# A fused attention and ELU-MLP kernel: preparing w_in moves to GpSimd, w_out is prepared two tiles at a time, the ELU is rewritten with a Relu on ScalarE, and the opening's order of work is new

## The chip, the cores and the metric

The kernel runs on one NeuronCore of a Trainium2 chip. The number that counts is the device time of one execution in microseconds (us). The engines are written as the profile names them: PE is TensorE (matmuls), PEld its weight loads, DVE VectorE, ACT ScalarE, POOL GpSimd, SP SyncE, which here only issues DMAs.

## The reference

`q`, `k` and `v` have shape (8 images, 12 heads, 448 tokens, 64) in float32. `w_in` (768 x 2048) and `w_out` (2048 x 768) come in float64, 12.6 MB each.

```python
scores = scale * np.matmul(q, k.transpose(0, 1, 3, 2)) - np.log(S)
attn = 1.0 / (1.0 + np.exp(-scores))
attn_out = np.matmul(attn, v)                       # sigmoid attention, no softmax
x = attn_out.transpose(0, 2, 1, 3).reshape(B * S, H * D)      # 3584 x 768
h = x @ w_in
g = np.where(h > 0.0, h, np.exp(np.minimum(h, 0.0)) - 1.0)    # ELU
out = g @ w_out
```

## The kernel before

**Arithmetic.** Most operands are split into a float16 high part and a float16 low part ("high" is a scaled copy on ACT, "low" is source times scale minus high on DVE, helper `low`, L186). A product is then three float16 matmuls. Only the six head pairs of image 0 are kept in float32 (`EXACT`); they are turned on PE (L483) and copied out of PSUM on DVE (`copied`, L490).

**Tiling.** The work goes by image. Per image there are six pairs of heads: `scores` (L549) gives a PSUM tile of 128 keys by 2 x 448 queries, `sigmoid` (L557) reads it on ACT, `values` (L619, L607) multiplies it with v, and `finish_high` and `finish_low` put the result into `xh`, the input of the MLP. The first layer (`moe1`, products at L723) walks over 16 tiles of 128 hidden units, 18 matmuls each, into PSUM tiles `ph`. For each, ACT takes the exponential (L733), DVE builds the ELU from it in two steps (L739, L740), ACT writes the high part of `g` (L746) and DVE its low part (L186). The second layer (`moe2`, L785) multiplies `g` with `w_out` into tiles of 128 tokens by 384 outputs, evicted on DVE (L795) and sent by SP (L799).

**The opening.** The weights must be turned from float64 into float16 pairs. A tile of 128 hidden units of w_in goes through these steps, one letter each in the string `ORDER`: `i` DMA of the raw words into a spare place of `wo` or `g` (L248); `A` two ACT passes, the top word's magnitude and the last bits (L202, L207); `B` DVE joins them (L211); `C` PE sums of magnitudes (L220); `D` a scale, by DVE and one small POOL step (L276, L141, L145); `E` DVE puts the sign back (L227); `F` ACT writes the high part (L288); `G` DVE the low part (L186, tile name `wi`). The float32 tile between `A` and `G` lies in one of five places (`stage`, `WT = 5`): the field of tile f+5 cannot start before `G` of tile f is done. w_out has the same steps in 32 tiles of 384 (`o`, `H` to `N`), staged in spare places of `wo` and in the buffers `at` and `o`.

**What sets the order.** The Tile layer here does not reorder: each engine runs its instructions in the order in which they are recorded, waiting on semaphores. In the opening that order is written out by hand: every letter of `ORDER` advances one generator of `streams`. The opening takes in all of image 0's and image 1's attention, all weights, and image 0's first and second layer (`m`, `x`, `y`, `z`, `w`, `p`). From the first layer of image 1 on, the order comes from the loop at the end of the kernel: the first layer of image b, then the attention of image b+1 with the matmuls of image b's second layer as filler between its steps.

## Time and profile before

| what | value |
|---|---|
| time of the runs | 1171.29 us median of 3 (1170.32 to 1171.38) |
| the profiled execution's own time | 1171.42 us |
| its span, first to last instruction | 1169.6 us |
| PE, PEld busy | 1141.7 us (98%), 635.5 us (54%) |
| DVE, ACT, POOL busy | 785.4 us (67%), 705.7 us (60%), 179.6 us (15%) |
| DMA | 92.12 MB, mean 79 GB/s; 254 to 266 GB/s in the first two slices of 29 us |

The two layers after the opening repeat for seven images at a PE that is busy throughout, so the page's shares over the whole span say little about the opening. The opening has to be cut out with windows: up to the first matmul of image 0's first layer, from there to the first of image 1's first layer, and the rest. An instruction's duration includes its pipeline's start and end, and neighbours on one engine overlap by some 0.08 us, so sums of durations are a little more than busy time.

### The profile page before, as it was taken

How to read it: one execution, taken by the hardware profiler on the slowest of the kernel's cores; microseconds unless marked ns; L12 is line 12 of the kernel's file. 1: busy time of each engine (PE TensorE's matmuls, PEld its weight loads, DVE VectorE, ACT ScalarE, POOL GpSimd, SP SyncE). 2: the span in 40 equal slices, each digit the busy share in tenths (PEclk: the TensorE clock that was granted, in tenths of full speed). 3: DMA queues.
4: the chain of work that ended last, by engine and by line, in shares of the span. 5: the costliest groups of instructions: out<-in, count | busy, mean ns of one | idle time of the engine just before them, and what ended most of it. 6: DMA issues, size and time to landing. Idle time of an engine off the chain costs nothing.

```text
span 1169.6 us, 23893 instructions
## 1 busy us (share of the span) xinstructions
PE 1141.7 (98%) x9662; PEld 635.5 (54%) x9662; DVE 785.4 (67%) x1506; ACT 705.7 (60%) x1087; POOL 179.6 (15%) x491
## 2 busy tenths in 40 slices
PE   5989999999999999999999999999999999999998
PEld 2335464555665555655666555655566555555565
DVE  6999988866666667866666666767576575855400
ACT  6987779746664368844766348845666446764300
POOL 1233212210220102211120111301022010300000
PEclk9999999999999999999999999999999999999999
DMA  9986445311242113512044121622134131310000
GB/s 254 266 259 209 124 98 112 86 41 42 63 95 63 41 42 78 120 28 62 19 99 96 38 50 42 110 55 52 39 84 92 37 60 30 73 36 1 1 27 27
DMA packets 219150, 92.12 MB, mean 79 GB/s; under 512 B 182688, under 2 KB 214944, under 8 KB 219040
## 3 DMA queue, kind: packets, MB, share of 16 engines
q1 hardware_dynamic: 219040, 90.61, 32.4%
q8 instruction: 75, 1.23, 0.4%
q14 instruction: 35, 0.29, 0.1%
HBM read 60.29 MB, written 11.01 MB: 61 GB/s over the span
## 4 chain that ended last, share of the span: by engine, by line
PE 81%; DVE 3%; ACT 2%; issue 1%; DMA 0%; POOL 0%; DVEq 0%; ACTq 0%; POOLq 0%
PE ph L723 33%; PE po L785 29%; PE pav L619 7%; PE psc L549 6%; PE po_r L785 5%; PE pscr L649 1%; ACT sg L557 1%; DVE wo L186 1%; DVE g L186 1%; DVE at L186 0%; DMA so<-in_moe_w_out_dram 0%; ACT at L587 0%; DVE nat L186 0%; ACT nat L501 0%; DVE mx L193 0%
## 5 line engine op out<-in xcount | busy, mean ns | idle before, releaser
L723 PE MATMUL ph<-xh,wi 128*128 128x448 f16 x2304 | 440.3, 352 | 1.0 <-DVE wi L186 0.9
L785 PE MATMUL po<-wo,g 128*64 128x384 f16 (+1 forms) x4320 | 393.0, 327 | 0.8 <-DVE e L740 0.5
L785 PEld LDWEIGHTS <-g 128*64 128x64 f16 (+1 forms) x4992 | 291.3, 109 | 160.1 <-issue 30.3
L723 PEld LDWEIGHTS <-wi 128*128 128x128 f16 x2304 | 223.4, 98 | 211.7 <-issue 3.7
L733 ACT ACTIVATE e<-ph,msc 128x448 f32<-128x448 f32 x128 | 81.0, 633 | 198.1 <-PE ph L723 168.4
L186 DVE SCALAR_TENSOR_TENSOR at<-sg,at 128x896 f16<-128x896 f32 x120 | 127.6, 1090 | 106.5 <-ACT at L587 106.5
L739 DVE TENSOR_SCALAR e<-e 128x448 f32<-128x448 f32 x128 | 50.1, 391 | 128.7 <-ACT e L733 128.7
L557 ACT ACTIVATE sg<-psc,bias,sc 128x896 f32<-128x896 f32 x126 | 133.9, 1094 | 3.1
L587 ACT ACTIVATE at<-sg 128x896 f16<-128x896 f32 x120 | 109.6, 947 | 0.7
L626 ACT ACTIVATE xh<-pav,sc 128x448 f16<-128x448 f32 x48 | 30.3, 632 | 127.7 <-PE pav L619 122.6
L746 ACT ACTIVATE g<-e,msc 128x384 f16<-128x384 f32 (+1 forms) x192 | 96.0, 533 | 6.7 <-DVE e L740 4.1
L186 DVE SCALAR_TENSOR_TENSOR g<-e,msc,g 128x384 f16<-128x384 f32 (+1 forms) x192 | 94.6, 522 | 0.4
L740 DVE SCALAR_TENSOR_TENSOR e<-ph,msc,e 128x448 f32<-128x448 f32 x128 | 87.5, 684 | 5.1
L549 PE MATMUL psc<-qk 64*128 64x448 f16 x756 | 86.3, 351 | 0.1
L145 POOL TENSOR_SCALAR sc<-sc 128x3 f32<-128x3 f32 (+1 forms) x48 | 11.7, 244 | 432.4 <-DVE pw L178 432.3
L619 PE MATMUL pav<-at,vn 128*64 128x448 f16 x720 | 75.6, 353 | 0.0
L619 PEld LDWEIGHTS <-vn 128*64 128x64 f16 x880 | 49.8, 110 | 32.2 <-issue 1.8
L785 PE MATMUL po_r<-wo,g 128*64 128x384 f16 (+1 forms) x672 | 64.9, 326 | 0.0
L186 DVE SCALAR_TENSOR_TENSOR nat<-raw,sc,nat 128x384 f16<-128x384 f32 (+1 forms) x126 | 60.0, 525 | 1.7 <-ACT nat L501 0.9
L501 ACT ACTIVATE nat<-raw,sc 128x384 f16<-128x384 f32 (+1 forms) x126 | 59.8, 531 | 1.3 <-POOL sc L145 0.9
L186 DVE SCALAR_TENSOR_TENSOR xh<-pav,sc,xh 128x448 f16<-128x448 f32 x48 | 32.6, 680 | 40.7 <-ACT xh L626 40.7
L795 DVE TENSOR_SCALAR o<-po,osc 128x384 f32<-128x384 f32 x48 | 29.3, 610 | 42.3 <-PE po L785 36.4
(120 smaller groups left out, 979.4 us busy)
## 6 DMA issues: line engine op xcount, KB each, us to landing
wo<-in_moe_w_in_dram SPq DMA_DIRECT2D x14, 768.0 KB, 6.3
raw<-in_q_dram SPq DMA_DIRECT2D x48, 192.0 KB, 3.9
raw<-in_k_dram SPq DMA_DIRECT2D x48, 192.0 KB, 3.4
rv<-in_v_dram SPq DMA_DIRECT2D x48, 192.0 KB, 3.0
out_dram<-o SPq DMA_DIRECT2D x48, 192.0 KB, 2.1
wo<-in_moe_w_out_dram SPq DMA_DIRECT2D x18, 384.0 KB, 3.8
so<-in_moe_w_out_dram SPq DMA_DIRECT2D x14, 384.0 KB, 3.7
rv<-in_v_dram SPq DMA_DIRECT2D x96, 32.0 KB, 2.5
```

Of the source, the lines that this page charges most:

```text
L186: nc.vector.scalar_tensor_tensor(lo, src, s, hi, op0=ALU.mult, op1=ALU.subtract)
L501: nc.scalar.mul(self.nat[:, 0, t : t + n], src, s)
L549: nc.tensor.matmul(psc[:, j, :S] if g < NC else psc[rows[j], 0, :S], kk[rows[j], o], qq[rows[j], :S], start=(n == 0), stop=(n == len(parts ...
L557: nc.scalar.activation(to, psc, AF.Sigmoid, bias=bias, scale=self.s_scale)
L587: nc.scalar.mul(hi, sg, 2.0**ATOP)
L619: nc.tensor.matmul(pav[rows[j], :S], vv[i][:, 2 * NC + j if g == NC else j * NC + g], sg[k][:, j], start=(g == 0 and n == 0), stop=(g == N ...
L723: nc.tensor.matmul(self.ph[f], wi[:, wj, c, f * P : (f + 1) * P], self.xh[c][:, xj], start=(n == 0), stop=(n == 3 * NK - 1),)
L733: nc.scalar.activation(self.e[f], self.ph[f], AF.Exp, scale=self.m[:, 0, f : f + 1])
L739: nc.vector.tensor_scalar(e, e, 1.0, -1.0, op0=ALU.min, op1=ALU.add)
L740: nc.vector.scalar_tensor_tensor(e, self.ph.pop(f), self.m[:, 0, f : f + 1], e, op0=ALU.mult, op1=ALU.max)
L746: nc.scalar.mul(g[:, 0, f, o : o + n], self.e[f][:, i : i + n], self.m[:, 1, f : f + 1])
L785: nc.tensor.matmul(po[r, :HM], tokens[:, r], wo[:, i, f, wj], start=(n == 0), stop=(n == 3 * NF - 1),)
```

## The change

The edits, by what they do:

- **w_in (F, G).** The staged float32 tile is scaled in place on POOL (`tensor_scalar`), copied into the high part on POOL (`tensor_copy`), and the low part is the difference of the two, on POOL again (`tensor_tensor`). ACT's scaled copy and DVE's `low` on w_in are gone.
- **Turned float32 pairs (e).** The copy out of PSUM for image 0's six pairs is made by ACT instead of DVE.
- **w_out (H to K).** Loads, fields, magnitudes, sums and signs take two 128-row tiles at once: 16 DMAs of 768 KB and 16 steps of 768 columns where 32 DMAs of 384 KB and 32 steps of 384 were. The splits (M, N) still go tile by tile. Raw words are staged in spare places of `wo` and `g` and, at the end, in `ats`.
- **ELU.** After the exponential, ACT computes Relu(c - c * exp(h)) in place, c being the inverse of the scale; DVE then takes max(h, 0) minus that in one step. The DVE step with `min` and `add` (L739) is gone. The scale table `msc` has three rows instead of two, each made by POOL, and `high` and `low` of g now use one scale per token image (`xr`) for all tiles.
- **Last keys of image 0.** The last 64 keys of two pairs share one PSUM tile, as for the other images.
- **Buffers.** `at` and `o` become fixed tiles (`ats`, `room`) with three places each.
- **End.** In the last image the tile of leftover tokens comes first in each half; the very last tile is evicted in two halves, DVE and ACT, each sent from its own queue (SP and ACT).
- **Order.** `ORDER` is another string, and k of the very first pair is loaded from ACT's queue.

```diff
 ORDER = (
-    "iiqviiqviAAAABCDEiBadbCFGcDeSEAABSCFGEiAABDCaDETTFSbSWTATAdWWWqviiFAXAAAGceBCSGEDBYYSCEa"
+    "iiiiiqqvvAAAAAAAAAABCDEBCEiiFGBDCDFEFGGBBCDCadCadbcEDEeSFGFGbceSTTASWWSTABAABSWCiiqiTAATD"
...
     def w_in_high():
         for f in range(NF):
-            nc.scalar.mul(wi[:, 0, :, f * P : (f + 1) * P], staged(f), w_in_scale[f])
+            t = staged(f)
+            nc.gpsimd.tensor_scalar(t, t, w_in_scale[f], None, op0=ALU.mult)
+            nc.gpsimd.tensor_copy(wi[:, 0, :, f * P : (f + 1) * P], t)
             yield
     def w_in_low():
         for f in range(NF):
             d = wi[:, :, :, f * P : (f + 1) * P]
-            low(d[:, 1], staged(f), w_in_scale.pop(f), d[:, 0])
+            nc.gpsimd.tensor_tensor(d[:, 1], staged(f), d[:, 0], op=ALU.subtract)
             yield
...
+                src = w_out[f * 2 * P : (f + 1) * 2 * P, i * HM : (i + 1) * HM]
+                nc.sync.dma_start(st, src.rearrange("(a p) c -> p a c", a=2))
...
+            issue = nc.scalar if i and b + hp == 0 else nc.sync
...
         def copied(self):
             qk = early[:, self.hp % 2]
-            nc.vector.tensor_copy(qk, self.pt[:, : 2 * S])
+            nc.scalar.copy(qk, self.pt[:, : 2 * S])
...
+        def missing(self, f):
+            e = self.e[f]
+            nc.scalar.activation(
+                e, e, AF.Relu, bias=self.m[:, 1, f : f + 1], scale=self.m[:, 2, f : f + 1]
+            )
         def elu(self, f):
             e = self.e[f]
-            nc.vector.tensor_scalar(e, e, 1.0, -1.0, op0=ALU.min, op1=ALU.add)
             nc.vector.scalar_tensor_tensor(
-                e, self.ph.pop(f), self.m[:, 0, f : f + 1], e, op0=ALU.mult, op1=ALU.max
+                e, self.ph.pop(f), 0.0, e, op0=ALU.max, op1=ALU.subtract
             )
...
+        def evict_halves():
+            (pp, dst), = dsts
+            turns["o"] += 1
+            o, h = room[:, turns["o"] % OB], HM // 2
+            nc.vector.tensor_scalar(o[:, :h], po[:, :h], sc(), None, op0=ALU.mult)
+            nc.scalar.mul(o[:, h:], po[:, h:HM], sc())
+            nc.sync.dma_start(dst[:, i * HM : i * HM + h], o[pp, :h])
+            nc.scalar.dma_start(dst[:, i * HM + h : (i + 1) * HM], o[pp, h:])
```

In what follows, line numbers of the changed kernel differ from those of before: L292, L293 and L299 are POOL's scale, copy and subtraction, L205 and L210 are ACT's field and last bits (L202 and L207 before), L560 is the sigmoid, L629 is `finish_high`, L747 the Relu.

The first place is POOL's queue at the start. Before, it holds only scales (`ws`, `sc`, `pw`, `xs`), one number a partition:

```order
L145 TENSOR_SCALAR ws<-ws 128x1
L145 TENSOR_SCALAR sc_0_157<-sc_0_157 128x1
L181 TENSOR_SCALAR pw_0_156<-pw_0_156 128x1
L418 COPY xs_164<-pw_0_156 128x1
L419 COPY xs_164<-sc_0_157 128x1
L421 TENSOR_SCALAR sc_0_157<-xs_164 128x1
L145 TENSOR_SCALAR ws<-ws 128x1 x3
```

Now three w_in tiles, nine instructions of 768 columns, stand ahead of the scales of the first pair:

```order
L148 TENSOR_SCALAR ws<-ws 128x1
L292 TENSOR_SCALAR g<-g,ws 128x768
L293 CAST wi<-g 128x6x128
L299 TENSOR_TENSOR wi<-g,wi 128x6x128
L148 TENSOR_SCALAR ws<-ws 128x1 x2
L292 TENSOR_SCALAR g<-g,ws 128x768
L293 CAST wi<-g 128x6x128
L292 TENSOR_SCALAR g<-g,ws 128x768
L293 CAST wi<-g 128x6x128
L299 TENSOR_TENSOR wi<-g,wi 128x6x128 x2
L148 TENSOR_SCALAR ws<-ws 128x1
L148 TENSOR_SCALAR sc_0_221<-sc_0_221 128x1
```

Each tile has become three wide instructions in this queue, in line with the small ones. Up to the field of the last w_in tile, eleven tiles must have passed.

The second place is ACT's queue at the end of image 0's attention (`psc` and `pscr` are score tiles, `pt` a turned pair, `xh` the MLP's input, `g<-wo` or `wo<-wo` 128x768 a weight tile). Before, from the fifth pair's high part (`pav_4`) to the sixth's:

```order
L626 ACTIVATE xh_173<-pav_4_662,sc_4_605 128x448
L557 ACTIVATE sg_5_762<-psc_5_738,bias 128x896
L202 ACTIVATE wo<-wo 128x384
L207 ACTIVATE wo<-wo 128x384
L557 ACTIVATE sg_5_766<-psc_5_741,bias 128x896
L557 ACTIVATE sg_5_792<-psc_5_782,bias 128x448
L202 ACTIVATE wo<-wo 128x384
L207 ACTIVATE wo<-wo 128x384
L202 ACTIVATE wo<-wo 128x384
L626 ACTIVATE xh_173<-pav_5_785,sc_5_689 128x448
```

Now, from the field of the last (16th) w_in tile on:

```order
L205 ACTIVATE g<-wo 128x768
L210 ACTIVATE wo<-wo 128x768
L560 ACTIVATE sgr_4_706<-pscr_4_694,bias 128x448
L560 ACTIVATE sg_5_739<-psc_5_717,bias 128x896
L629 ACTIVATE xh_239<-pav_4_665,sc_4_609 128x448
L210 ACTIVATE g<-g 128x768
L560 ACTIVATE sg_5_788<-psc_5_782,bias 128x896
L560 ACTIVATE sg_5_790<-psc_5_785,bias 128x896
L205 ACTIVATE wo<-wo 128x768
L210 ACTIVATE wo<-wo 128x768
L205 ACTIVATE wo<-wo 128x768
L629 ACTIVATE xh_239<-pav_5_792,sc_5_682 128x448
```

The scaled copies of w_in (L288) have left this queue and the copies of turned pairs (`pt`, L494) have come in further up. The last pair's high part still stands behind a fixed list of weight passes, and the 16th field now stands behind POOL's eleventh subtraction.

The third place is the end: SP's last DMAs before, of the leftover tokens (two parts),

```order
L799 DMA out_0_dram<-o7_2_1_14529 128x384
L799 DMA out_0_dram<-o7_r_1_14581 64x384 x2
```

and ACT's last rows now, its half of the last eviction and the DMA of it:

```order
L821 ACTIVATE room_72<-po7_2_1_14283,osc6_12340 128x192
L823 DMA out_0_dram<-room_72 128x192
```

SP has the other half, one DMA of 128 rows by 192 columns, instead of two DMAs one after the other.

More of the change, by code (lines that the diff above doesn't have):

```diff
@@ L103, in attention_ffn @@
     early = early.rearrange("p (n x) -> p n x", n=2)
+    ats = const.tile([P, AB, 2, 2, S], F16, name="ats")
+    turns = {"at": 0, "o": 0}
+    room = const.tile([P, OB, HM], F32, name="room")
     wp = const.tile([P, NF], F32, name="wp")
@@ L376, in w_out_low @@
             s = w_out_scale[i][:, 1 + f : 2 + f]
[L377 removed]
+            low(wo[:, i, f, 1], w_out_whole[i, f // 2][:, f % 2], s, wo[:, i, f, 0])
             yield
@@ L386, in load_qk @@
         for i, src in enumerate((q, k)):
-            nc.sync.dma_start(
+            issue = nc.scalar if i and b + hp == 0 else nc.sync
+            issue.dma_start(
                 raw[:, i * (NC + 1) :][:, :NC],
@@ L390, in load_qk @@
             )
-            nc.sync.dma_start(
+            issue.dma_start(
                 raw[rows[i], NC], src[b, h0 : h0 + 2, SM:].rearrange("h r d -> r h d")
@@ L549, in scores @@
                     nc.tensor.matmul(
-                        psc[:, j, :S] if g < NC else psc[rows[j], 0, :S],
-                        kk[rows[j], o], qq[rows[j], :S],
+                        psc[:, j, :S], kk[rows[j], o], qq[rows[j], :S],
                         start=(n == 0), stop=(n == len(parts) - 1),
@@ L559, in soften @@
         def soften(self, g):
-            nb = 2 if g < NC else 1
             psc = self.psc.pop(g)
             sg = sb.tile([P, 2, S], F32, tag="sg", name=f"sg{g}{self.u}", bufs=SB)
-            self.sigmoid(sg[:, :nb], psc[:, :nb, :S])
+            self.sigmoid(sg, psc[:, :, :S])
             self.sg[g] = [sg]
@@ L584, in high @@
             (sg,) = self.sg[g]
-            at = sb.tile([P, 2, 2, S], F16, tag="at", name=f"at{g}{self.u}", bufs=AB)
+            at = ats[:, turns["at"] % AB]
+            turns["at"] += 1
             hi, lo = at[:, 0], at[:, 1]
@@ L643, in last_keys @@
         o = slice(S, S + R)
-        for n in range(3):
+        terms = 2 * len(two[0].qk) - 1
+        for n in range(terms):
             for i, p in enumerate(two):
-                hi, lo = p.qk
+                hi, lo = p.qk[0], p.qk[-1]
                 kk, qq = [(hi, hi), (lo, hi), (hi, lo)][n]
@@ L773, in moe1, with moe2_tile @@
         x.parts(NF - 1)
-    def moe2_tile(dsts, lh, sc, i, u, halves, out_later=None):
+    def moe2_tile(dsts, lh, sc, i, u, halves, out_later=None, last=False):
         cols = slice(i * HM, (i + 1) * HM)
@@ L793, in evict @@
         def evict():
-            o = sb.tile([P, HM], F32, tag="o", name=f"o{u}", bufs=OB)
+            turns["o"] += 1
+            o = room[:, 2 if turns["o"] <= NC else turns["o"] % OB]
             nc.vector.tensor_scalar(o, po[:, :HM], sc(), None, op0=ALU.mult)
@@ L831, in tokens, with tile_of @@
             return out[b * S + SM : (b + 1) * S]
-        def tile_of(c, i):
+        def tile_of(c, i, last):
             if c < NC:
@@ L846, in moe2 @@
         for i in range(NH):
-            for c in range(NC + j):
-                yield from tile_of(c, i)
+            tiles = list(range(NC + j))
+            if b == B - 1:
+                tiles = tiles[NC:] + tiles[:NC]
+            for c in tiles:
+                yield from tile_of(c, i, b == B - 1 and (c, i) == (NC - 1, NH - 1))
     pairs = [(b, hp) for b in range(B) for hp in range(NP)]
@@ L950, in scores @@
             p = pair_of(n)
-            for t in range(NC + (n < FIRST)):
+            for t in range(NC):
                 p.scores(t)
@@ L954, in scores @@
                 yield
-            if n >= FIRST and n % 2 == 0:
+            if n % 2 == 0:
                 two = pair_of(n), pair_of(n + 1)
@@ L1005, in layer @@
         xp, xr, last = next(whole)
-        m = sb.tile([P, 2, NF], F32, tag="msc", name=f"msc{b}")
+        m = sb.tile([P, 3, NF], F32, tag="msc", name=f"msc{b}")
         def first():
@@ L1095, in attention_ffn @@
         "m": first_layer("products"), "x": first_layer("exponential"),
-        "y": first_layer("elu"), "z": first_layer("high"), "w": first_layer("low"),
+        "l": first_layer("missing"), "y": first_layer("elu"), "z": first_layer("high"), "w": first_layer("low"),
         "p": output_products(), "k": evictions(),
```

119 lines of the change are left out of this document (59 added, 60 removed).

## The prediction

> **What bounds the kernel now.** I cut the span by windows at three instants: the first `ph` matmul of image 0 (85.3 us), the first of image 1 (226.8), and PE's end (1165.4). The columns are the window, its length, busy time of PE, PEld, DVE, ACT and POOL with instruction counts, PE clock, DMA share and GB/s.
>
> ```profile
> 0.00:30.00 30.00, 17.10 (x82) 7.98 (x84) 18.20 (x36) 18.41 (x23) 5.17 (x23) 0.94 0.94 253
> 30.00:85.30 55.30, 47.77 (x266) 18.21 (x263) 52.45 (x108) 50.06 (x71) 16.07 (x41) 0.97 0.97 273
> 85.30:226.80 141.50, 138.22 (x1166) 76.16 (x1166) 132.02 (x263) 115.60 (x194) 35.07 (x72) 1.00 0.51 127
> 226.80:1165.40 938.60, 938.57 (x8154) 533.14 (x8153) 582.10 (x1101) 521.62 (x801) 123.32 (x356) 1.00 0.25 55
> 1165.40:1169.60 4.20, 0.00 (x0) 0.00 (x0) 0.62 (x1) 0.00 (x0) 0.00 (x0) 0.92 0.20 47
> ```
>
> From 226.8 us on PE is idle for 0.03 of 938.6 us, so nothing on another engine can shorten that stage; it can only lengthen it. From 85.3 to 226.8 PE is idle for 3.3 us. Before 85.3 PE has little to do that is ready; there DVE (52.45 of 55.30 us), ACT (50.06) and the DMA engines (0.97) are all nearly full. After it, PE has a fixed list: 16 tiles of the first layer, the second layer and image 1's attention. So the time is the instant of the first `ph` matmul, plus a list that PE works off almost without a gap, plus the tail. PE's timeline shows that instant and the next one:
>
> ```profile
> 85.28 3.56 PE L723 MATMUL ph<-xh,wi 128*128 128x448 f16 x18
> 226.78 3.58 PE L723 MATMUL ph<-xh,wi 128*128 128x448 f16 x18
> ```
>
> **What the change does before 85.3 us.** By lines, up to that instant, first ACT's groups and then DVE's (count, busy us, mean ns, idle before):
>
> ```profile
> L557 ACT ACTIVATE sg<-psc,bias 128x896 f32<-128x896 f32 x18 | 17.6, 1000 | 0.6 <-PE psc L549 0.6
> L202 ACT ACTIVATE g<-wo 128x768 f32<-128x768 f32 x14 | 12.6, 899 | 6.1 <-DMA wo<-in_moe_w_in_dram 6.1
> L288 ACT ACTIVATE wi<-g,ws 128x768 f16<-128x768 f32 x12 | 11.1, 929 | 2.9 <-POOL ws L145 2.8
> ...
> L202 ACT ACTIVATE wo<-wo 128x384 f32<-128x384 f32 x6 | 3.3, 556 | 0.0
> ```
> ```profile
> L227 DVE SCALAR_TENSOR_TENSOR g<-wo,g 128x768 uint32<-128x768 uint32 x14 | 13.3, 953 | 1.5 <-PE si L220 1.5
> L211 DVE SCALAR_TENSOR_TENSOR g<-g,wo 128x768 uint32<-128x768 uint32 x14 | 13.3, 954 | 6.0 <-ACT wo L207 5.9
> L186 DVE SCALAR_TENSOR_TENSOR wi<-g,ws,wi 128x768 f16<-128x768 f32 x11 | 11.1, 1012 | 0.0
> L490 DVE COPY g<-pt 128x896 f32<-128x896 f32 x6 | 6.5, 1084 | 2.9 <-PE pt L483 2.9
> ```
>
> DVE loses 11.1 + 6.5 = 17.6 of 70.7 us and stops being a bound. ACT loses 11.1 us of scaled copies and gains six copies out of PSUM; this ACT form is not in the trace, but a sigmoid of the same size from PSUM is (17.6 / 18 = 0.98 us), so +5.9. A w_out field of two tiles costs one 768-wide pass (0.90) where two of 0.56 were, a gain of 0.2 a pass, which in this stage, with about ten passes, is some 0.4 us after overlap. ACT goes from 68.5 to 62.9 us. If ACT paced the stage at the same busy share, the instant would be 85.3 x 62.9 / 68.5 = 78.3: 7.0 us earlier.
>
> POOL sets the other bound. A tile of w_in now takes three of its instructions, and the field of tile 16 on ACT waits for the subtraction of tile 11. No POOL instruction this wide is in the trace. The nearest rows:
>
> ```profile
> 0.72 0.10 POOL L88 MEMSET bias<- 128x1 f32 x1 [0.29 <-POOLq L1201]
> 0.75 0.20 POOL masks.py:197 MEMSET ident<- 128x128 f32 x1
> 1.31 0.29 POOL masks.py:199 TENSOR_SCALAR_AFFINE_SELECT ident<-ident 128x128 f32<-128x128 f32 x1
> 13.18 0.22 POOL L181 TENSOR_SCALAR pw<-pw 128x1 f32<-128x1 f32 x1
> ```
>
> From 1 to 128 columns a memset grows by 0.10 us, 0.8 ns a column; the select, which also reads, by 1.5 ns at most. With 0.2 us fixed, 768 columns are 0.84 us at the one rate and 1.36 at the other. I take 0.84 for scale and copy, and for the subtraction, with two inputs read in turn, twice the column rate: 1.5. A tile then takes 3.2 us when nothing disturbs it (2.5 if the second input is free, 5.2 at the select's rate throughout). The Trainium skill (GPSIMD Engine Reference, Elementwise — side-by-side cycle accounting) gives 4.5 us for a two-input add of 2048 float32 columns; an estimate by it is 1.7 us for the subtraction, and the tile would be 3.4 us.
>
> It is disturbed. In the steady stage POOL's small steps and DVE's stand so in time (start, length; POOL, then DVE):
>
> ```profile
> 304.28 1.19 POOL L465 COPY sc<-sc 64x1 f32<-64x1 f32 x2
> 305.57 0.64 POOL L467 TENSOR_SCALAR sc<-pw 128x1 f32<-128x1 f32 x1
> 306.31 0.59 POOL L415 TENSOR_SCALAR xs<-xs,pw 128x1 f32<-128x1 f32 x1
> ```
> ```profile
> 304.34 1.09 DVE L186 SCALAR_TENSOR_TENSOR at<-sg,at 128x896 f16<-128x896 f32 x1 [0.54 <-ACT at L587]
> 305.46 1.27 DVE L577 SCALAR_TENSOR_TENSOR ar<-sgr,ar 64x448 f16<-64x448 f32 x2
> ```
>
> A POOL step of about 0.2 us that meets a DVE step with two SBUF inputs ends just after that step does (305.47 after 305.43; 306.21 after 306.1, the end of the first of the two at 305.46): it waits for the rest of it. The Trainium skill (SBUF — State Buffer, Summary: rules for kernel authors) says that whichever of the two starts second is blocked entirely; the trace agrees for POOL behind DVE (1.19 us for two steps of 0.2), and no run here shows the other direction with a long POOL step. This speaks against the change: magnitudes and signs (L211, L227) are such DVE steps, 34.6 us of them before 85.3 with the w_out ones. The wait per POOL instruction lies between nothing and one whole DVE step (0.95 us), so 0 to 2.85 a tile. DVE spends 34.6 of 85 us, 0.4, in such steps, and the mean rest of one is 0.47, which gives 0.6; with DVE often eager, I take 1.1. The tile is then 4.3 us (2.5 to 8.1 between the far ends).
>
> POOL can start where the first scaled copy does now (10.4 us), and 31 small steps stand in its queue up to the eleventh subtraction, at 0.33 us each (21.24 us in 64 instructions before 85.3) 10.3 us. The rows of that start and of the last pair's high part, which stands 2.9 us ahead of the first `ph`:
>
> ```profile
> 10.40 0.94 ACT L288 ACTIVATE wi<-g,ws 128x768 f16<-128x768 f32 x1 [1.01 <-POOL ws L145]
> ...
> 82.35 0.64 ACT L626 ACTIVATE xh<-pav,sc 128x448 f16<-128x448 f32 x1 [2.58 <-PE pr L171]
> ```
>
> Eleven tiles end at 10.4 + 11 x 4.3 + 10.3 = 68.0 us. From the 16th field ACT has eleven passes to the last pair's high part (six weight passes of 0.9, three sigmoids of 1.0, one of 0.6 and one high part of 0.6), 8.8 us after overlap, and it waits for PE's value products there, which I take as the 2.58 us of now: 79.4. With the 2.9 us that follow the instant is 82.3, **-3.0 us**. POOL, not ACT, sets it.
>
> **After it.** DVE is busy for 132.0 of 141.5 us and loses 16 ELU steps (0.39 each, 6.2 us), the last five low parts of w_in (4.7) and some 4 us by w_out's wider steps. ACT is at 115.6; it gains 16 Relus and loses four scaled copies and about 5 us of fields. A Relu of 448 columns I price like the exponential, 0.64:
>
> ```profile
> L733 ACT ACTIVATE e<-ph,msc 128x448 f32<-128x448 f32 x112 | 71.1, 635 | 194.6 <-PE ph L723 167.0 <-PE pr L171 25.9 <-POOL msc L697 1.4
> L739 DVE TENSOR_SCALAR e<-e 128x448 f32<-128x448 f32 x112 | 43.9, 392 | 128.7 <-ACT e L733 128.7
> ```
>
> Both stay under PE's list, and at most PE's 3.3 us of idling come back. I take **-1.0**. Bounds: -3.3, and +3 if new waits of the same kind open.
>
> In the steady stage ACT gains 112 x 0.635 = 71 us and DVE loses 43.9. ACT would be at 593 of 938.6. For each `ph` tile ACT has exponential, Relu and high part, 1.9 us (2.2 where the high part is in two), against PE's 3.56 for the 18 matmuls; the ELU's chain grows by 0.24 us under the two tiles that PE is ahead. **0**. Without that lead it would cost 0.24 x 112 = 27 us. POOL's third step per image delays only the first Relu of an image, behind three further `ph` tiles. The buffers `ats` and `room` keep three places.
>
> **The tail.**
>
> ```profile
> 1165.41 0.62 DVE L795 TENSOR_SCALAR o_r<-po_r,osc 128x384 f32<-128x384 f32 x1 [7.18 <-PE po_r L785]
> 1166.05 1.11 SPq L799 DMA_DIRECT2D out_dram<-o_r  x2
> ```
>
> Half of the eviction lies between 0.31 and 0.62; at 0.45 it saves 0.17. The second issue, half of 1.11, goes to ACT's queue: 0.55. **-0.7** (0 to -0.9).
>
> **Sum.** Against the profiled execution's 1171.4: -3.0 - 1.0 + 0 - 0.7 = -4.7, so 1166.7; its time is 0.13 above the median of the runs, so **1166.6**.
>
> **The rivals.**
>
> *A. POOL is later, and the change is slower.* If every POOL instruction meets a whole DVE step, a tile is 6.05 us, eleven end at 87.3, and the first `ph` comes at 101.6: +16.3. Break-even is at 4.6 us a tile. For a middle value of 5.2, the instant is 92.2, +6.9; with the tail's -0.7: 1177.5. For it speaks 1.19 us for two short copies above; against it, DVE's lower load. Its mirror, DVE held up by POOL, makes fields and signs late and ends the same.
>
> *B. POOL is quick and meets few DVE steps.* At 3.2 us a tile ACT is the bound at 78.3; with the most of the rest (-7.0 - 2.0 - 0.7) this gives 1161.6. For it speaks that DVE's load falls by a quarter (17.6 of 70.7 us), so that fewer POOL steps find it busy; against it, that what stays on DVE is mostly of the two-input kind.
>
> *C. No change.* The DMA engines are at 0.97 up to 85.3 us and their bytes are the same. Five w_in tiles now go ahead of the first q, so the first sigmoid comes later than now and ACT's gain is eaten by its early idling (6.1 us already wait for w_in): the instant stays, and with the tail 1170.
>
> **How the numbers follow.** The forecast has 0.42, B 0.13, C 0.18, A 0.27. About 0.2% (2.3 us) is what a measurement of this kernel tells from no change: faster 0.55, same 0.18, slower 0.27. The range is 1159 to 1178: from a little beyond B, if PE's idling comes back in full, to A's middle value; A's far end is left out. The likeliest case alone has 1163 to 1169.
>
> **What would show it.** Right: the first `ph` near 82; wide POOL steps of 0.8 to 1.7 us whose ends lie just behind DVE steps; ACT's fields waiting for POOL's subtraction; PE without a gap from image 1 on; a tail near 3.5 us. Wrong: a tile over 4.6 us, DVE's signs stretched beyond 0.95 us, the first sigmoid much after 18 us, or PE waiting for the ELU.

## The result, and the profile after

The changed kernel takes 1193.72 us (median of 4 runs, 1192.79 to 1193.87); the kernel before, run beside it, takes 1171.34. The ratio is 1.0186, with a 95% interval of 1.0173 to 1.0200. It is slower, by 22 us, where 5 us less had been forecast. The profiled execution took 1192.79 us with a span of 1191.0.

These are the windows of the changed kernel, cut at the same events as in the prediction: 30 us, the first `ph` matmul of image 0, the first of image 1, PE's end, the end. The columns are those of the prediction's first table.

```profile
0.00:30.00 30.00, 13.85 (x85) 8.04 (x86) 16.86 (x34) 18.56 (x23) 20.50 (x23) 1.00 0.98 275
30.00:103.85 73.85, 51.33 (x260) 19.36 (x258) 45.34 (x83) 46.54 (x58) 69.96 (x72) 0.83 0.71 191
103.85:247.43 143.58, 139.94 (x1171) 74.85 (x1169) 126.94 (x218) 118.45 (x180) 51.71 (x94) 0.99 0.49 120
247.43:1186.80 939.37, 939.37 (x8154) 533.16 (x8153) 535.11 (x991) 605.36 (x913) 123.18 (x363) 1.00 0.25 56
1186.80:1191.00 4.20, 0.02 (x1) 0.00 (x0) 0.42 (x1) 0.42 (x1) 0.00 (x0) 1.00 0.16 49
```

The first `ph` matmul starts at 103.85 us instead of 85.28, 18.6 us later. From there to image 1's first the kernel takes 2.1 us more (143.6 against 141.5), the steady stage 0.8 more (939.4 against 938.6), the tail 0.05 less. The sum, 21.4, is the difference of the spans (1191.0 and 1169.6). In the second window DVE and ACT are no longer full (45 and 47 of 74 us), nor is DMA (0.71, before 0.97). POOL is: 69.96 of 73.85 us.

POOL's wide steps, by lines over the whole run (count, busy us, mean ns, idle before), and the small scale that every w_in tile needs, by lines from 0 to 120 us:

```profile
L292 POOL TENSOR_SCALAR g<-g,ws 128x768 f32<-128x768 f32 x16 | 39.8, 2485 | 0.6
L299 POOL TENSOR_TENSOR wi<-g,wi 128x768 f16<-128x768 f32 x16 | 30.0, 1887 | 0.7
L293 POOL CAST wi<-g 128x768 f16<-128x768 f32 x16 | 16.3, 1020 | 1.1
```
```profile
L148 POOL TENSOR_SCALAR ws<-ws 128x1 f32<-128x1 f32 x16 | 9.6, 601 | 9.3 <-DVE ws L144 8.0
```

A tile takes 2485 + 1020 + 1887 = 5392 ns of POOL. The chain of waits of the changed kernel up to the first `ph`, in order of time (start, length, work), runs through POOL almost without a break from 33.5 to 95 us. Its end:

```profile
84.79 2.23 POOL wi L299
...
88.74 2.97 POOL g L292
91.78 0.97 POOL wi L293
92.83 0.80 POOL ws L148
...
94.75 0.27 POOL xs L420
...
95.32 2.11 DVE xh L676 x4
...
99.76 2.10 DVE wo L214
101.86 0.60 DVE xh L189
```

The eleventh subtraction ends at 87.02. Then the scale and copy of a later tile stand in POOL's queue ahead of the last pair's small steps (`ws` at 92.83 to `xs` at 94.75). DVE's rescaling of the other five parts of `xh` (L676) waits for those, and the last low part (L189) stands behind it in DVE's queue, with a w_out step between them (99.76) that takes 2.10 us, more than twice its usual 0.95, beside a subtraction on POOL. The waits up to 110 us say who stands behind POOL:

```profile
PE si L223 <- DVE g L214: 20.9, 7, 8.2
DVE g L214 <- ACT wo L210: 20.7, 6, 6.0
ACT g L205 <- POOL wi L299: 16.4, 5, 6.1
```

The columns are us in total, times and longest. ACT's field waits for POOL's subtraction 16.4 us, DVE's magnitudes wait for ACT, and PE's sums for DVE: one wait, passed on twice.

PE's timeline around the first `ph`, and two windows that show its clock (the third number from the end) there:

```profile
102.51 1.44 PE L223 MATMUL so<-wo,ones 128*128 128x384 bf16 x4 [5.69 <-DVE xh L189]
103.85 4.98 PE L730 MATMUL ph<-xh,wi 128*128 128x448 f16 x18
```
```profile
100.00:105.00 5.00, 2.49 (x9) 1.11 (x9) 4.93 (x7) 1.51 (x2) 5.00 (x3) 0.50 0.24 58
105.00:110.00 5.00, 5.00 (x24) 2.44 (x23) 4.90 (x9) 1.07 (x1) 4.76 (x4) 0.83 0.57 157
```

PE was idle for 5.69 us, its granted clock was 0.50 and then 0.83, and the first 18 `ph` matmuls took 4.98 us where 3.56 stood before. That is 1.4 of the 2.1 us lost between the two first `ph`.

### The profile page after: what moved, and what is told of

Read it like the earlier page. It is cut to its first block, busy times and chain, and to the rows that moved or that the text cites. A ratio compares the mean times of both kernels' runs of the same rounds, so it can differ in the third digit from the quotient of the medians.

```text
span 1191.0 us, 23762 instructions
## 1 busy us (share of the span) xinstructions
PE 1144.5 (96%) x9662; PEld 635.4 (53%) x9662; DVE 724.7 (61%) x1324; ACT 789.3 (66%) x1174; POOL 265.3 (22%) x550
## 4 chain that ended last, share of the span: by engine, by line
PE 85%; POOL 5%; DVE 4%; ACT 3%; DMA 2%; issue 1%; SPq 0%; DVEq 0%; POOLq 0%; ACTq 0%
PE ph L730 32%; PE po L796 31%; PE pav L622 7%; PE psc L553 7%; PE po_r L796 5%; POOL g L292 2%; POOL wi L299 1%; PE pscr L653 1%; POOL wi L293 1%; DVE wo L230 1%; DMA wo<-in_moe_w_in_dram 1%; DMA qk<-nat 1%; DVE wo L214 1%; POOL ws L148 0%; DVE mx L196 0%
## 5 line engine op out<-in xcount | busy, mean ns | idle before, releaser
L753 DVE SCALAR_TENSOR_TENSOR e<-ph,e 128x448 f32<-128x448 f32 x128 | 79.6, 622 | 183.2 <-ACT e L747 183.2
L189 DVE SCALAR_TENSOR_TENSOR ats<-sg,ats 128x896 f16<-128x896 f32 x120 | 127.4, 1089 | 104.4 <-ACT ats L590 104.4
L560 ACT ACTIVATE sg<-psc,bias,sc 128x896 f32<-128x896 f32 x126 | 133.7, 1093 | 5.9 <-PE psc L553 2.7
L629 ACT ACTIVATE xh<-pav,sc 128x448 f16<-128x448 f32 x48 | 30.3, 631 | 121.3 <-PE pav L622 120.0
L590 ACT ACTIVATE ats<-sg 128x896 f16<-128x896 f32 x120 | 109.5, 947 | 0.6
L747 ACT ACTIVATE e<-e,msc 128x448 f32<-128x448 f32 x128 | 97.4, 761 | 4.4
L759 ACT ACTIVATE g<-e,rr 128x384 f16<-128x384 f32 (+1 forms) x192 | 95.4, 531 | 2.7 <-DVE e L753 2.2
L189 DVE SCALAR_TENSOR_TENSOR g<-e,rr,g 128x384 f16<-128x384 f32 (+1 forms) x192 | 95.5, 527 | 0.4
L622 PE MATMUL pav<-ats,vn 128*64 128x448 f16 x720 | 75.9, 353 | 0.5 <-DVE xh L189 0.5
L189 DVE SCALAR_TENSOR_TENSOR nat<-raw,sc,nat 128x384 f16<-128x384 f32 (+1 forms) x126 | 60.6, 529 | 1.5 <-ACT nat L505 0.7
L452 POOL TENSOR_TENSOR mx<-mx,half 128x2 bf16<-128x2 bf16 x42 | 10.5, 250 | 218.5 <-DVE mx L196 211.7
L189 DVE SCALAR_TENSOR_TENSOR xh<-pav,sc,xh 128x448 f16<-128x448 f32 x48 | 32.6, 680 | 43.0 <-ACT xh L629 43.0
```

The source lines that it names most:

```text
L189: nc.vector.scalar_tensor_tensor(lo, src, s, hi, op0=ALU.mult, op1=ALU.subtract)
L560: nc.scalar.activation(to, psc, AF.Sigmoid, bias=bias, scale=self.s_scale)
L590: nc.scalar.mul(hi, sg, 2.0**ATOP)
L622: nc.tensor.matmul(pav[rows[j], :S], vv[i][:, 2 * NC + j if g == NC else j * NC + g], sg[k][:, j], start=(g == 0 and n == 0), stop=(g == N ...
L747: nc.scalar.activation(e, e, AF.Relu, bias=self.m[:, 1, f : f + 1], scale=self.m[:, 2, f : f + 1])
L753: nc.vector.scalar_tensor_tensor(e, self.ph.pop(f), 0.0, e, op0=ALU.max, op1=ALU.subtract)
```

## The experiments

The theory that the profile suggests, P: POOL's time per tile of w_in sets the first `ph`. Rivals: the new order itself is worse (O); what counts is that POOL's wide steps hold DVE up (D); the Relu form costs (R). "First `ph`", "image 0" (from the first `ph` to image 1's first) and "steady" are from the profiled execution of each run, in us; the time is the median. POOL's time per tile is the sum of the mean durations of its wide steps. The interval is that of the ratio to runs of the kernel before taken beside it. e14's profiled execution is the slowest of its ten (1174.8).

| run | order | w_in on POOL | time | ratio (95%) | first `ph` | image 0 | steady |
|---|---|---|---|---|---|---|---|
| before | old | nothing | 1171.3 | | 85.3 | 141.5 | 938.6 |
| the change | new | all, 5.39 us a tile | 1193.7 | 1.0173 to 1.0200 | 103.8 | 143.6 | 939.4 |
| e2 | old | all, 5.24 | 1197.6 | 1.0215 to 1.0247 | 104.8 | 148.9 | 938.6 |
| e17 | old | every second tile | 1182.9 | 1.0075 to 1.0114 | 93.4 | 145.5 | 938.6 |
| e18 | old | every fourth tile | 1176.0 | 1.0023 to 1.0053 | 87.4 | 144.6 | 938.6 |
| e5 | new | narrow scale, 3.89 | 1178.6 | 1.0039 to 1.0088 | 89.9 | 143.2 | 939.4 |
| e6 | new | narrow scale and subtraction, 2.67 | 1166.9 | 0.9945 to 0.9969 | 81.6 | 141.9 | 939.4 |
| e1 | new | nothing | 1191.2 | 1.0159 to 1.0198 | 100.2 | 145.6 | 939.4 |
| e16 | new | every fourth tile | 1188.4 | 1.0131 to 1.0165 | 99.3 | 144.5 | 939.4 |
| e15 | new | every second tile | 1187.7 | 1.0123 to 1.0153 | 96.6 | 147.1 | 939.4 |
| e11 | new | nothing, all on DVE | 1180.5 | 1.0060 to 1.0108 | 93.5 | 141.2 | 939.4 |
| e14 | old | nothing; Relu alone | 1172.1 | 1.0001 to 1.0024 | 87.0 | 142.4 | 939.4 |

**Is POOL alone enough? (e2)** The kernel before, in its old order, with only w_in's three steps put on POOL:

```diff
-            nc.scalar.mul(wi[:, 0, :, f * P : (f + 1) * P], staged(f), w_in_scale[f])
+            t = staged(f)
+            nc.gpsimd.tensor_scalar(t, t, w_in_scale[f], None, op0=ALU.mult)
+            nc.gpsimd.tensor_copy(wi[:, 0, :, f * P : (f + 1) * P], t)
...
-            low(d[:, 1], staged(f), w_in_scale.pop(f), d[:, 0])
+            nc.gpsimd.tensor_tensor(d[:, 1], staged(f), d[:, 0], op=ALU.subtract)
```

> The kernel before with one part of the change alone: w_in's scale, copy and subtraction on GpSimd, in the old order. Theory P: eleven tiles at 5.4 us and the small steps end near 80 us and the old order was not made for that; the first ph comes at 96 to 108 us and the time is 1182 to 1195 us. Rival O: the first ph stays within 4 us of 85.3, the time under 1176 us.

It took 1197.6 us. POOL's lines up to 105 us, and PE's row of the first `ph`:

```profile
L289 POOL TENSOR_SCALAR g<-g,ws 128x768 f32<-128x768 f32 x13 | 31.7, 2437 | 0.6
L296 POOL TENSOR_TENSOR wi<-g,wi 128x768 f16<-128x768 f32 x11 | 19.2, 1753 | 0.5
L290 POOL CAST wi<-g 128x768 f16<-128x768 f32 x12 | 12.6, 1051 | 0.8
```
```profile
104.77 5.24 PE L725 MATMUL ph<-xh,wi 128*128 128x448 f16 x18
```

The first `ph` comes 19.5 us late without any other part of the change, and the time is a little beyond P's upper end. POOL alone is enough.

**How much of it does POOL bear? (e17, e18)** The same, but only the odd tiles (e17), or only tiles 3, 7, 11 and 15 (e18), go to POOL; the others stay as before. e18's condition is shown; e17 has `f % 2`:

```diff
+            if f % 4 == 3:
+                nc.gpsimd.tensor_scalar(t, t, w_in_scale[f], None, op0=ALU.mult)
+                nc.gpsimd.tensor_copy(wi[:, 0, :, f * P : (f + 1) * P], t)
+            else:
+                nc.scalar.mul(wi[:, 0, :, f * P : (f + 1) * P], t, w_in_scale[f])
...
+            if f % 4 == 3:
+                nc.gpsimd.tensor_tensor(d[:, 1], staged(f), d[:, 0], op=ALU.subtract)
+            else:
+                low(d[:, 1], staged(f), w_in_scale.pop(f), d[:, 0])
```

> The kernel before, its order kept, with every second tile of w_in (the odd ones) on POOL. Output is the reference's. P: the first ph moves in proportion to POOL's share above what fits: with all tiles on POOL it came 19.5 us later, with half of them 0 to 8 us later (85 to 93), time 1168 to 1182. If this old order suffers at once from any long POOL step (each small scale on POOL that q and k wait for stands behind it), half of the loss: first ph 95, time 1184.

> As the run before, with every fourth tile (3, 7, 11, 15) on POOL. P: ACT loses 3.7 us and DVE 4 us before the first ph, POOL has some 16 us more and is not full: first ph 82 to 87, time 1167 to 1173, the one version of this series that could beat the kernel before. If any long POOL step costs in proportion: a quarter of 26 us, time 1178.

They took 1182.9 and 1176.0 us, with the first `ph` 8.1 and 2.1 us later than before. With a share of 0, 1/4, 1/2 and all, the ratio goes 1, 1.0038, 1.0095, 1.0231: no share gains. e18 lies outside what P expected (1167 to 1173) and nearer the other answer (1178); e17 lies just beyond P's upper end. A POOL with room to spare still costs. In e18 this is not the small steps behind the wide ones: up to 90 us POOL itself waits 33.9 us for DVE's `ws`, and ACT's wait for POOL's `ws` hardly grew (3.6 us, before 2.8). The timelines of DVE and POOL show another cause:

```profile
45.44 1.59 DVE L227 SCALAR_TENSOR_TENSOR g<-wo,g 128x768 uint32<-128x768 uint32 x1
51.02 2.35 DVE L211 SCALAR_TENSOR_TENSOR g<-g 128x768 uint32<-128x768 uint32 x1
```
```profile
45.32 2.24 POOL L290 TENSOR_SCALAR g<-g,ws 128x768 f32<-128x768 f32 x1
50.91 1.65 POOL L300 TENSOR_TENSOR wi<-g,wi 128x768 f16<-128x768 f32 x1
```

DVE is nearly full in the old order, and four of its steps (at 29.80, 45.44, 47.94 and 51.02) take 7.1 us beside POOL's wide ones where 3.9 is their usual length. DVE's copies of turned pairs, 0.4 us later than before at 26.8 us, are 2.7 us later at 62.7. So D is at work in the old order. The rest of e18's loss lies behind the first `ph`, where the first 18 matmuls take 5.10 us instead of 3.56.

**What is dear in a tile? (e4, e5, e6)** In the changed kernel the scale is by a fixed number (e4), or is cut to 128 of the 768 columns (e5), or scale and subtraction both are (e6, where the unwritten low parts are zeroed at the start, half of them on POOL):

```diff
-            nc.gpsimd.tensor_scalar(t, t, w_in_scale[f], None, op0=ALU.mult)
+            nc.gpsimd.tensor_scalar(t, t, 2.0, None, op0=ALU.mult)                          # e4
+            nc.gpsimd.tensor_scalar(t[:, 0], t[:, 0], w_in_scale[f], None, op0=ALU.mult)    # e5, e6
...
-            nc.gpsimd.tensor_tensor(d[:, 1], staged(f), d[:, 0], op=ALU.subtract)
+            nc.gpsimd.tensor_tensor(d[:, 1, 0], staged(f)[:, 0], d[:, 0, 0], op=ALU.subtract)    # e6
```

> The changed kernel with GpSimd's scale of w_in by a fixed number (2.0) instead of each tile's own scale: the weights are then scaled wrongly and the output is not the reference's; the work is otherwise the same. If the 2.2 us of a scale come from reading the factor through an operand per partition, the step falls to 0.8 to 1.0 us, a tile to 4 us and the first ph to 84 to 92 us. If they belong to this instruction as such, the step stays at 2.2 us and the first ph at 102 to 106 us.

> The changed kernel with GpSimd's scale on 128 of a tile's 768 columns; the other columns of w_in stay unscaled, so that the output is not the reference's. Copy and subtraction are whole. Theory P (GpSimd's length sets the pace): a tile falls from 5.4 to some 3.5 us, eleven tiles end 20 us earlier, near 67 us; the first ph comes at 82 to 88 us, the time is 1170 to 1177 us. Rival O (the new order is itself late, as the run with w_in back on ACT and DVE may say): the first ph stays at 95 us or later, the time at 1184 us or more.

> The changed kernel with scale and subtraction on GpSimd on 128 of 768 columns (the rest of the low parts is set to zero at the start, and the output is not the reference's); the copy is whole. Theory P: a tile takes GpSimd some 2 us, ACT and the DMA queues set the pace; the first ph comes at 76 to 84 us, the time is 1163 to 1172 us, and ACT's fields no longer wait for GpSimd. Rival O: the first ph stays at 95 us or later.

e4, one run: 1192.5 us, first `ph` at 102.7. POOL's lines of e4 (up to 104 us), e5 (with two of DVE's) and e6 (up to 105):

```profile
L292 POOL TENSOR_SCALAR g<-g 128x768 f32<-128x768 f32 x14 | 34.0, 2428 | 0.5
```
```profile
L299 POOL TENSOR_TENSOR wi<-g,wi 128x768 f16<-128x768 f32 x14 | 26.3, 1884 | 0.7
L292 POOL TENSOR_SCALAR g<-g,ws 128x128 f32<-128x128 f32 x14 | 15.6, 1117 | 0.6
L293 POOL CAST wi<-g 128x768 f16<-128x768 f32 x14 | 12.4, 887 | 0.9
L230 DVE SCALAR_TENSOR_TENSOR g<-wo,g 128x768 uint32<-128x768 uint32 x14 | 17.0, 1223 | 0.9 <-PE si L223 0.9
L214 DVE SCALAR_TENSOR_TENSOR g<-g,wo 128x768 uint32<-128x768 uint32 x14 | 16.6, 1188 | 9.5 <-ACT wo L210 7.3 <-POOL ws L148 1.7 <-issue 0.3
```
```profile
L294 POOL TENSOR_SCALAR g<-g,ws 128x128 f32<-128x128 f32 x14 | 16.0, 1145 | 0.6
L295 POOL CAST wi<-g 128x768 f16<-128x768 f32 x14 | 13.5, 966 | 0.9
L301 POOL TENSOR_TENSOR wi<-g,wi 128x128 f16<-128x128 f32 x14 | 7.8, 563 | 0.7
```

The scale by a number takes 2428 ns: its price belongs to the instruction, not to the operand of one number per partition. (That it works in place and writes float32, where the copy writes float16, was not varied.) With one order and one set of other work, 5.39, 3.89 and 2.67 us a tile give a first `ph` at 103.8, 89.9 and 81.6. That is a dose and its answer, and P is shown for this order. It is shown apart from D too: e5 keeps the copy and the subtraction, and DVE's signs and magnitudes stay as long as in the change (17.0 and 16.6 us, there 17.5 and 15.9), yet 14.0 of the 18.6 us come back. e5 landed a little above P's range. e6 landed in it, and, with part of the work left out, is the only run faster than before. But its chain of waits shows that POOL no longer sets that instant:

```profile
61.51 6.41 DMA wo<-in_moe_w_in_dram
...
73.75 4.93 DMA rv<-in_v_dram
```

With POOL quick, the loads decide. Its eleventh subtraction ends at 58.7, and the 16th field starts at 68.0, when its words have landed.

**Can another engine take the dear step? (e3, e10, e13, e11)** All in the new order. e3: the scale on DVE. e10: also the small bound of `ws`, so that DVE's scale needn't wait for POOL. e13: high part, scale and bound on DVE, only the subtraction on POOL. e11: high and low part and bound on DVE, nothing wide on POOL.

```diff
-            twice_inverse(ws[:, f : f + 1], m, TINY * 2.0 ** (1 - WTOP))
+            nc.vector.tensor_scalar(...)      # e10, e11, e13: both steps of the bound on DVE
...
-            nc.gpsimd.tensor_scalar(t, t, w_in_scale[f], None, op0=ALU.mult)
+            nc.vector.tensor_scalar(t, t, w_in_scale[f], None, op0=ALU.mult)      # e3, e10, e13
...
-            nc.gpsimd.tensor_copy(wi[:, 0, :, f * P : (f + 1) * P], t)
+            nc.vector.tensor_scalar(wi[:, 0, :, f * P : (f + 1) * P], t, w_in_scale[f], None, op0=ALU.mult)   # e11, e13
...
-            nc.gpsimd.tensor_tensor(d[:, 1], staged(f), d[:, 0], op=ALU.subtract)
+            low(d[:, 1], staged(f), w_in_scale.pop(f), d[:, 0])      # e11
```

> The changed kernel with the scale of w_in (in place, 768 columns) on DVE, copy and subtraction still on GpSimd. Theory P, with the scale (2.2 us alone) as the mis-sized term: a tile takes GpSimd 0.8 + 1.6 us and some 0.9 of waits, 3.4 in all, GpSimd no longer sets the pace; the first ph comes at 80 to 88 us, the time is 1166 to 1175 us. Rival L (the port that GpSimd and DVE take in turn is the cause, not the scale's own length): copy and subtraction hold it as before and DVE has one step more, the first ph stays over 95 us, the time over 1182 us.

> The changed kernel with w_in's scale step (in place) and the small step that bounds each tile's factor both on DVE; copy and subtraction on GpSimd. The earlier run with the scale alone on DVE came to 1190.9 us, with DVE waiting 7.9 us for GpSimd's small step and GpSimd 18.9 us for DVE's scale. Theory P with coupling: without that round trip GpSimd has 2.5 us and waits a tile, as in the run with a narrow scale or less; the first ph comes at 82 to 90 us, the time is 1167 to 1178 us. Rival L (copy and subtraction hold the port that DVE needs): the first ph stays over 95 us, the time over 1184 us.

> The changed kernel with only the subtraction on GpSimd (1.6 us alone): high part and scale in place are two DVE steps, the factor's bound is on DVE. Theory P: GpSimd has 2 us a tile, the first ph comes at 80 to 87 us, the time is 1165 to 1174 us, the lowest of the versions that compute the reference. Rival L: the first ph stays over 92 us, the time over 1180 us.

> The changed kernel with nothing wide on GpSimd: w_in's high part a scaled copy on DVE, its low part DVE's step as before, the factor's bound on DVE too. ACT keeps the relief that the change gives it. DVE has some 1.4 us a tile more than in the changed kernel, 73 of 85 us. Theory P: the first ph comes at 84 to 90 us, the time is 1169 to 1177 us. Rival O (the new order is late without GpSimd too): over 1184 us, as with w_in back on ACT and DVE (1191.2).

They took 1190.9 (ratio 1.0156 to 1.0194), 1186.0 (1.0107 to 1.0151), 1193.1 (1.0162 to 1.0214) and 1180.5 us, with the first `ph` at 100.7, 96.2, 101.9 and 93.5. POOL had 3.01, 3.08, 1.94 and 0 us a tile, so here POOL's time alone doesn't order the results. The traces show waits at the hand-over between the engines. The waits of e3 (up to 100 us) and of e13 (up to 93 us):

```profile
POOL wi L293 <- DVE g L292: 18.9, 6, 5.9
DVE g L292 <- POOL ws L148: 7.9, 3, 5.9
```
```profile
POOL wi L307 <- DVE g L301: 41.2, 11, 13.1
```

Between two queues that work in order, each step of a tile waits for the other engine's turn. In e3 POOL waits 18.9 us for DVE's scale, in e13 41.2 us. e11, where no tile changes hands between these two, is the quickest of the four. All four missed what P expected of them, which was made with POOL's time alone. e3, e10 and e13 lie where rival L put them (copy and subtraction hold DVE up). In e3 that explains little: up to 100 us DVE's signs and magnitudes take 29.4 us together, 2.8 more than before, while the first `ph` is 15.4 us late. That the hand-over is the reason is read from the waits; e11 takes away the hand-over and POOL's work together.

**Is the new order itself at fault? (e1, e15, e16)** The changed kernel with w_in back on ACT and DVE (e1: the two edits of e2 the other way round), or with every second (e15) or every fourth (e16) tile left on POOL (the edits of e17 and e18).

> The changed kernel with one part undone: w_in's high part is ACT's scaled copy again and its low part DVE's step (order, w_out in pairs, Relu, copies of turned pairs and the end stay as changed). Theory P (GpSimd's three wide steps a tile, 5.4 us measured, hold up the 16th field and with it the first ph matmul, 103.8 us instead of 85.3): the first ph comes back to 84 to 90 us, the time to 1170 to 1177 us. Rival O (the new order is at fault: five w_in tiles ahead of the first q, w_out in steps of two): the first ph stays over 98 us, the time over 1186 us. Rival R (the Relu form of the ELU costs the time behind the first ph): the first ph comes back but the time stays over 1180 us.

> The changed kernel, its order kept, with only every second tile of w_in (the odd ones) on POOL; the even ones are made as before, high part by a scaled copy on ACT, low part on DVE. Output is the reference's. Theory P (POOL's time a tile sets the first ph): POOL's mean per tile falls from 5.4 to about 2.7 us, below the 3.6 that gave a first ph at 89.9; ACT and DVE carry some 6 us more than in the changed kernel; first ph 84 to 90, time 1169 to 1176. Rival O (the new order fits only a w_in that is wholly on POOL; any tile that ACT and DVE make in it stands in the way of their other work): first ph 92 to 101 as where all tiles were made elsewhere, time 1180 to 1191.

> As the run with every second tile, but only every fourth tile (3, 7, 11, 15) on POOL. P: POOL 1.35 us a tile; nothing on POOL is late, ACT and DVE are nearly as loaded as before; first ph 84 to 90, time 1169 to 1176. O: nearer to the run with no tile on POOL (first ph 100.2): 95 to 100, time 1184 to 1191; so O expects this run to be slower than the one with every second tile, P about equal.

They took 1191.2, 1187.7 and 1188.4 us, with the first `ph` at 100.2, 96.6 and 99.3. All three miss P's ranges and fall where O expected them. The longest wait of e1 up to 100 us:

```profile
POOL ws L148 <- DVE ws L144: 51.8, 10, 10.6
```

In e1 POOL waits for DVE, not the other way round. The first sigmoid stands at 35.5 us (34.1 in e15, 34.0 in e16, 23.1 in the change, 17.7 before): the new order puts five tiles of w_in ahead of the first q, and where ACT and DVE make these tiles, the first scores wait behind them. So the new order doesn't fit a w_in made by ACT and DVE. It isn't tied to POOL either: with w_in wholly on DVE (e11) it is at 1.0084, while the change is at 1.0186, and e2, with neither the order nor the other parts, at 1.0231. Putting w_in back while keeping the order doesn't undo the loss.

**The rest of the change (e7, e8, e14).** e7 takes the rest of the change without POOL's part, in the old order with the letters of w_out halved; in e8 DVE copies the turned pairs again. Both compute something else, probably because the wide w_out loads of the new code land in places whose w_in words haven't all been read in this order, and they may carry waits that neither kernel has.

```diff
 ORDER = (
+    the old string, the letters of the w_out streams halved
...
-            nc.gpsimd.tensor_scalar(t, t, w_in_scale[f], None, op0=ALU.mult)
-            nc.gpsimd.tensor_copy(wi[:, 0, :, f * P : (f + 1) * P], t)
+            nc.scalar.mul(wi[:, 0, :, f * P : (f + 1) * P], staged(f), w_in_scale[f])
...
-            nc.scalar.copy(qk, self.pt[:, : 2 * S])
+            nc.vector.tensor_copy(qk, self.pt[:, : 2 * S])      # e8 only
```

> The kernel before's order (letters of w_out halved, a Relu after each exponential) with the rest of the change: w_out in pairs, Relu form of the ELU, turned pairs copied by ACT, fixed buffers, the end in halves. w_in stays on ACT and DVE, last keys and loads as before. If only GpSimd's part is at fault, the first ph comes at 82 to 88 us and the time is 1166 to 1174 us. If the Relu form, the wide w_out steps or the copies on ACT cost time of their own, the time is over 1178 us.

> As the run before it, with the turned pairs copied by DVE as in the kernel before. If ACT's copies block fields behind them in ACT's queue, this one is 2 to 6 us faster than it, 1164 to 1170 us; if ACT's room covers them, the two agree within 2 us.

They took 1195.3 (ratio 1.0183 to 1.0224) and 1191.5 us (1.0157 to 1.0192), with the first `ph` at 94.0 and 89.8 and 158 us from there to image 1's. As they don't compute the same, the pair says nothing of the rest as a whole. Its one use is the difference: with the copies on ACT the kernel is 3.8 us slower than with them on DVE, within the 2 to 6 us expected of copies that block the fields behind them.

e14 is the kernel before with the Relu form of the ELU alone.

```diff
+            nc.scalar.activation(e, e, AF.Relu, bias=self.m[:, 1, f : f + 1], scale=self.m[:, 2, f : f + 1])
...
-            nc.vector.tensor_scalar(e, e, 1.0, -1.0, op0=ALU.min, op1=ALU.add)
             nc.vector.scalar_tensor_tensor(
-                e, self.ph.pop(f), self.m[:, 0, f : f + 1], e, op0=ALU.mult, op1=ALU.max
+                e, self.ph.pop(f), 0.0, e, op0=ALU.max, op1=ALU.subtract
             )
```

> The kernel before with the Relu form of the ELU alone (a Relu after each exponential on ACT, one DVE step less, three rows of scales), old order. The stage from image 1 on has PE without a gap in the changed kernel as well; so the time stays within 1169 to 1174 us. Rival R: ACT's longer queue delays image 0's second layer or the sigmoids, the time is over 1176 us.

1172.1 us (10 runs), ratio 1.0001 to 1.0024: at most a quarter of a per cent, and R is no cause of 1.9%. Of the 0.8 us that the steady stage lost, all is in e14 (939.4) and none in e2 (938.6), with PE busy throughout in both: it belongs to the Relu form, and why PE's list grows by it is open.

No version with the whole computation beat the kernel before. What the rest of the change would give in an order made for it, with w_in on ACT and DVE, is open too.

## Why the prediction was wrong

**The frame held.** The time is the instant of the first `ph` plus a list that PE works off. From the forecast's sum of 1166.7 to the profiled 1192.8 it is +21.5 at that instant (103.8 instead of 82.3), +3.1 between the two first `ph` (+2.1 instead of -1.0), +0.8 in the steady stage and +0.65 in the tail.

**The step that failed: POOL's tile at 4.3 us.** It takes 5.39, and 5.27 in the first eleven tiles, on which the sum rests. Of the 21.5 us at the first `ph`, these eleven make 10.7 (58.0 us instead of 47.3), the small steps and gaps among them 8.1 and the way from there to the first `ph` 2.5; POOL's later start is the rest. Rival A had the mechanism, the direction and the size (5.2 us as its middle, a first `ph` at 101.6 at its far end), though it put the time down to waits for DVE. That was a minor part: the shortest durations of the three steps are already 2.20, 0.82 and 1.64, in sum 4.66, where 3.2 was priced.

- The scale is the mis-sized term: 0.84 was taken, 2.2 measured (2.5 with waits), 15 us too little over eleven tiles. The waits, too high, took back some 5 of them. It was priced by the column rate of a memset. The same operation stood in the trace of before, with fewer columns; this row (POOL's lines by form) was not used:

```profile
L697 POOL TENSOR_SCALAR msc<-wp,xs 128x16 f32<-128x16 f32 x7 | 1.9, 278 | 0.0
```

   A one-column scale there takes 0.22 us (the prediction's row at 13.18). Fifteen more columns add 58 ns, 3.9 ns a column: an estimate of 0.22 + 767 x 0.0039 = 3.2 us for the scale, with two factors instead of one. The measured 2.2 us is 2.6 ns a column. The upper end of the tile's bounds (8.1) had room for this; the value chosen hadn't.
- The copy was right: 0.84 priced, 0.82 at its shortest. The subtraction was nearly right: 1.5 priced, 1.64 measured.
- The Trainium skill (GPSIMD Engine Reference, Elementwise — side-by-side cycle accounting) gave an estimate of 1.7 us for the subtraction, and the trace agrees with its 1.64. The Trainium skill (the same page, Engine selection) calls one-input operations on GpSimd roughly line-rate; the copy agrees (0.82 us for 768 columns) and the scale doesn't, at 2.7 times the copy's duration.

**The waits between POOL and DVE** were priced at 1.1 us a tile in one direction. They are 0.73 us a tile (5.39 - 4.66; 0.61 in the first eleven), and they go in both directions, which no row of before could show. The timelines of POOL and of DVE from 33 to 38 us of the changed kernel:

```profile
33.51 2.22 POOL L292 TENSOR_SCALAR g<-g,ws 128x768 f32<-128x768 f32 x1
35.80 0.82 POOL L293 CAST wi<-g 128x768 f16<-128x768 f32 x1
```
```profile
34.42 0.95 DVE L230 SCALAR_TENSOR_TENSOR g<-wo,g 128x768 uint32<-128x768 uint32 x1
36.07 1.37 DVE L230 SCALAR_TENSOR_TENSOR g<-wo,g 128x768 uint32<-128x768 uint32 x1
```

The second DVE step starts during the copy (35.80 to 36.62) and takes 1.37 us instead of 0.95: it waits for the copy's rest. The same timelines from 10 to 17 us, POOL's rows and then DVE's:

```profile
10.62 2.92 POOL L292 TENSOR_SCALAR g<-g,ws 128x768 f32<-128x768 f32 x1
...
14.93 1.64 POOL L299 TENSOR_TENSOR wi<-g,wi 128x768 f16<-128x768 f32 x1
```
```profile
10.48 0.96 DVE L214 SCALAR_TENSOR_TENSOR g<-g,wo 128x768 uint32<-128x768 uint32 x1
...
15.45 1.94 DVE L230 SCALAR_TENSOR_TENSOR g<-wo,g 128x768 uint32<-128x768 uint32 x1
```

Behind the subtraction DVE's step takes 1.94. DVE's lines up to 108 us give the sum:

```profile
L230 DVE SCALAR_TENSOR_TENSOR g<-wo,g 128x768 uint32<-128x768 uint32 x14 | 17.5, 1258 | 0.9 <-PE si L223 0.9
L214 DVE SCALAR_TENSOR_TENSOR g<-g,wo 128x768 uint32<-128x768 uint32 x14 | 15.9, 1143 | 20.9 <-ACT wo L210 20.7
```

Signs and magnitudes took 17.5 and 15.9 us where 13.3 each stood before, so 6.8 us of the 17.6 that DVE was to be relieved of went back. The Trainium skill (SBUF — State Buffer, Summary: rules for kernel authors) says that whichever starts second is blocked; for copy and subtraction the trace now agrees in this direction too (1.37 and 1.94 us instead of 0.95).

**Small steps of 10.3 us before the eleventh subtraction.** From POOL's first wide step (10.62) to the end of the eleventh subtraction (87.02) are 76.4 us; the eleven tiles take 58.0 of them, and 18.4 are left: 30 small steps with 15.6 us, 0.52 each, and 2.8 of gaps. The priced 0.33 was the mean of a queue that includes the short memsets of the start. A small scale of `ws` took 601 ns in the mean (527 before) where 205 to 220 is its length alone.

**14.3 us from there to the first `ph`, through ACT.** It was 16.8, and the chain shows another way: not ACT's passes but the scale and copy of a further tile (88.74 to 92.75), which POOL's queue has ahead of the last pair's small steps, and then DVE's queue behind those. The prediction counted the small steps that the wide ones wait for, and not the wide ones that the small steps wait for.

**Break-even at 4.6 us a tile** was therefore too high. e5, at 3.89, is still slower than before; e6, at 2.67, is faster. e6's first `ph` at 81.6 and its 1166.9 us are almost the forecast's 82.3 and 1166.6, but with loads as the bound: the numbers agree, the reason doesn't.

**Rival C's point** was true as well: the first sigmoid came at 23.1 us instead of 17.7. It didn't decide, since in e6 it comes at 23.3 and the first `ph` is early.

**Between the first `ph` of image 0 and of image 1** the forecast had -1.0 and +3 as its bound for new waits; 1.4 of the 2.1 us are a cause that it hadn't, PE's clock after the idle time.

**The Relu** was priced like the exponential, 0.64. From SBUF it takes 0.76 (L747, 128 of them in 97.4 us). Two tiles of lead cover it, as forecast: PE is busy for all of 939.37 us.

**The tail** was to gain 0.7 and gained 0.05. Its timeline:

```profile
1186.86 0.42 DVE L820 TENSOR_SCALAR room<-po,osc 128x192 f32<-128x192 f32 x1 [7.18 <-PE po L796]
1187.64 0.42 ACT L821 ACTIVATE room<-po,osc 128x192 f32<-128x192 f32 x1 [60.21 <-DVE room L820]
```

The half was priced well (0.42 against 0.45), but ACT's half starts only after DVE's: two halves one after the other, and the second issue behind them. That alone isn't the reason: e1, e15 and e16 end in the same two halves, one after the other, and their tails are the 3.5 us of the forecast, with 0.08 us between the halves in e1 (0.36 here). With the same end the tails go from 3.5 to 4.4 us (e4); why is open.
